# Last sums of the spectral filter's pairs 6 and 7 in layer 2 by TensorE, and a new order of the loads, in a two-layer spectral and dense kernel

## The chip, the cores and the metric

One core of a Trainium2 chip runs the whole program. The metric is the device time of one execution in microseconds, taken as the median of several runs.

## The reference

The input has 2048 rows of 448 values in bfloat16. Two layers are the same, each a spectral part (A) and a dense part (B) with a residual.

```python
def _A_ref(x, w_r, w_i):
    X = rfft2(x.astype(float32), axes=(-2, -1))
    X = X * (w_r + 1j * w_i)
    y = irfft2(X, s=(S, D), axes=(-2, -1)).astype(bfloat16)
    return y

def _B_ref(x, w1, b1, w2, b2):
    h = x @ w1 + b1
    r = where(h > 0, h, 0)
    return (r * r) @ w2 + b2

x = x + _A_ref(_layernorm(x), w_r, w_i)
x = x + _B_ref(_layernorm(x), w1, b1, w2, b2)
x = x + _A_ref(_layernorm(x), w_r, w_i)
x = x + _B_ref(_layernorm(x), w1, b1, w2, b2)
```

S is 2048, D is 448, the dense part's width is 1792. The filter w has one complex value for each of the 2048 x 225 frequencies; its first column does not matter, as the mean is taken out.

## The kernel before

Rows are held as 128 partitions by 16 tiles. The Fourier transform over the 2048 rows is split into 16 x 128, so that all of it is matrix multiplication with constants. The stages of a spectral part are:

- first_A or second_A: a tile of x, times a constant matrix FA scaled by the row's normalisation factor (Fs), goes to XA. GpSimd and ScalarE scale in layer 1; GpSimd also makes a reversed copy of x for it (xr, held in VT).
- stage_TD: the transform over the 448 columns, constants TD in layer 1 and TQ in layer 2, result U.
- stage_B: the rest of the transform over the rows, constants G, result EF. From here on the 16 parts of the first split are taken in pairs p = 1 to 7, and pair 0 apart. A pair p has the complex spectra of two conjugate row groups.
- stage_W: the filter. For pairs, VectorE multiplies EF by w (rows tmp<-arena,Wt), subtracts and adds the products (T[3], rows tmp<-tmp), and forms the difference and the sum of the two conjugate halves, the "last sums" (rows arena<-tmp), which are written to Z. Pair 1 is done alone, the pairs 2 and 3, 4 and 5, 6 and 7 together, and pair 0 last.
- stage_Bi: the inverse over rows, for a pair two passes (even and odd columns, lb). In a pass, four matmuls have a 128 x 128 part of Z as the stationary operand and 256 columns of the constant H as the moving one. The result is copied from PSUM to VT by ScalarE or VectorE: 1024 elements at once for pairs 1 to 5 (MERGE), 512 for a pass of the pairs 6 and 7, and twice 256 for a pass of pair 0.
- stage_TI and stage_AI: the inverse over columns and the rest of that over rows; then the residual is added (L1146), the normalisation follows (ln_B), and yT holds x transposed: by matmuls for tiles 0 and 1, by DMA transposes on SP's queue for the others.

The dense part (h_part, h_pairs, o_tile) is long runs of matmuls, with ReLU on ScalarE, the square on VectorE, and the residual by VectorE's scalar_tensor_tensor (L1292). The last tile's output comes in two parts, 336 and 112 columns, and each part is stored by its own DMA.

Every engine runs a list written out by hand: ORDER holds, for each engine, numbers of units in the order in which they run. A unit is one instruction, or a group of matmuls that write one tile of PSUM, numbered in the order in which the program creates them. All waits follow from the data. Where TensorE would idle for long, matmuls on a tile of ones are put in (L1415). These numbers are of use below (numbering of before):

- SP: 3, 6, 8, 10 are x loads of two tiles each (tiles 0, 4, 8 and 12 first); 4 is FA, 28 TD, 30 GN (negated G), 29 G for the pairs, 36 and 37 the filter for pair 0, 31 and 32 the filter for the pairs, 38 TI, 33 and 35 H, 44 to 47 the dense weights, 269 TQ. ScalarE's queue loads the other four pieces of x.
- VectorE, layer 1: 167, 168, 200 copy 448 elements of U, 172 copies 448 of EF, 186 copies 896 of U; 173 is the first filter step; 246 the last. 258, 260, 262 copy 512 elements to VT, and 266, 268 twice 256.
- ScalarE, layer 1: 319, 337, 357, 375, 393, 411 are copies of 896 elements for stage_TI, 305 one for tiles 2 and 3; 279 and 283, 296 and 300 copy yT of tiles 0 and 1.
- Layer 2: 922 to 929 are the eight filter steps of pairs 6 and 7 (928 and 929 the last sums), 934 to 937 those of pair 0. Matmul units 948 and 950 are pair 6, 952 and 954 pair 7, 956 and 958 pair 0; the copies to VT after them have the next number up.
- The end: matmul units 1342, 1345, 1348 are tiles 12, 13 and 14, and 1351 and 1354 the 336 and 112 columns of tile 15.

Two helpers issue nearly all that the profile shows: matmuls have line 681, copies from PSUM 706 (ScalarE) or 707 (VectorE), sums and products of two tensors 735, loads 673. In the profile's names, U, EF, Z and the dense part's buffers are views of arena; yA, TIo of tmp; xr of VT; W1 and W2 are W_sb.

Of the kernel before, what the change touches and what calls it, by code (L numbers as in the profile page):

```python
# [6 lines left out]
ALU = mybir.AluOpType  # L7
# [4 lines left out]
P = 128  # L12
# [12 lines left out]
VB_PAIRS = (2, 3, 4, 5)  # L25
MERGE = (1, 2, 3, 4, 5)
# [10 lines left out]
def make_constants():  # L37
# [70 lines left out]
    return dict(GN=GN, FA=np.concatenate([FA, -FA], 1), FI=np.concatenate([FI, -FI], 1), TD=TD, G=G, H=H, TI=TI, TQ=TQ,  # L108
# [18 lines left out]
1354""",  # L127
    "act": """
# [12 lines left out]
1315 1325 1323 1330 1328 1335 1333 1338 1340""",  # L141
    "dve": """
# [24 lines left out]
    "pool": """  # L167
12 14 16 15 13 18 17 20 19 22 69 21 26 61 77 85 23 24 106 93 25 116 132 129 158 155 145 142""",
    "sp": """
3 4 6 8 36 38 10 34 31 27 35 28 29 39 30 41 32 33 37 44 47 45 40 46 314 269 334 352 354 355 372 390 408 426 1005 1026  # L170
1044 1046 1064 1082 1047 1100 1118 1250 1209 1306 1303 1203 1212 1253 1259 1300 1297 1350 1206 1347 1256 1344 1353
1356""",
}
# [1320 lines left out]
```

## Time and profile before

| | us |
|---|---|
| median of 3 runs | 266.54 |
| lowest and highest | 266.14, 266.84 |
| the profiled execution | 266.92 |
| its span, first to last instruction | 265.0 |
| TensorE busy in the span | 256.8 |
| VectorE busy | 204.5 |
| ScalarE busy | 172.7 |
| GpSimd busy | 14.2 |

The granted TensorE clock is 1.000 over the span. A matmul's busy time includes its way through the array, so matmuls that follow one another overlap; the distance of their starts is the price of one, not the mean length. In a timeline row, the first number is the start, the second the time from the first start to the last end, x the count, and the bracket holds the idle time ahead of it and what ended it.

### The profile page before, as it was taken

Reading aid. Unit: us, or ns where it says so; the run is one execution under the profiler, and the core shown is the slowest. Engines: PE = TensorE matmul, PEld = TensorE weight load, DVE = VectorE, ACT = ScalarE, POOL = GpSimd, SP = SyncE. Lnnn points to the kernel's source line nnn. Section 1 sums busy time; section 2 is a strip of 40 time slices with the busy share of each in tenths; the row PEclk is TensorE's granted clock in tenths of the full one; section 3 lists DMA queues with packets and bytes.
Section 4 is the critical chain, followed back from the end, with each engine's and each line's share of the span. In section 5 each row is a group of like instructions: output and inputs, shape, how many; then the busy total and the mean of one; then the engine's idle time right before and its main releaser. Section 6 shows DMA issues by size and latency. Waiting matters only on the chain.

```text
span 265.0 us, 5666 instructions
## 1 busy us (share of the span) xinstructions
PE 256.8 (97%) x2125; PEld 162.6 (61%) x2125; DVE 204.5 (77%) x658; ACT 172.7 (65%) x375; POOL 14.2 (5%) x32
## 2 busy tenths in 40 slices
PE   6999989999999999999999999999999999999996
PEld 2676768797544555665558756789654465554454
DVE  2978998999969983489998899899964069921662
ACT  5978897999449447893216889999634886121820
POOL 8840000000000000000000000000000000000000
PEclk9999999999999999999999999999999999999999
DMA  7999900032300214000000000022232000220053
GB/s 223 303 299 385 270 8 2 0 72 41 74 2 1 44 37 80 2 0 2 0 1 2 2 0 2 0 45 41 42 69 45 2 0 2 40 41 2 0 173 106
DMA packets 25531, 16.33 MB, mean 62 GB/s; under 512 B 18174, under 2 KB 24542, under 8 KB 25504
## 3 DMA queue, kind: packets, MB, share of 16 engines
q1 hardware_dynamic: 24768, 14.25, 19.9%
q10 hardware_dynamic: 576, 0.92, 1.0%
q0 software_dynamic: 160, 0.81, 0.9%
q8 instruction: 17, 0.28, 0.4%
q14 instruction: 10, 0.08, 0.1%
HBM read 10.46 MB, written 1.84 MB: 46 GB/s over the span
## 4 chain that ended last, share of the span: by engine, by line
PE 81%; DVE 8%; ACT 5%; DMA 2%; issue 2%; SPq 0%; POOL 0%; DVEq 0%; POOLq 0%
PE ps L681 81%; DVE tmp L735 6%; DMA xin<-in_A_x_dram 2%; DVE arena L735 2%; ACT VT L706 2%; ACT tmp L706 2%; ACT arena L706 1%; SPq L673 0%; ACT yT L706 0%; ACT mv L700 0%; DVE st L825 0%; PE ps L1415 0%; ACT Fs L717 0%; POOL Fs L718 0%; DVE VT L707 0%
## 5 line engine op out<-in xcount | busy, mean ns | idle before, releaser
L681 PE MATMUL ps<-yT,W_sb 64*128 64x512 bf16 (+1 forms) x770 | 90.3, 346 | 0.1
L681 PE MATMUL ps<-W_sb,arena 128*128 128x448 bf16 (+3 forms) x476 | 87.0, 342 | 0.0
L681 PEld LDWEIGHTS ps<-yT,W_sb 64*128 64x128 bf16 (+1 forms) x770 | 54.5, 95 | 31.9 <-ACT arena L700 1.3
L700 ACT ACTIVATE arena<-ps,b1col 128x512 bf16<-128x512 f32 x84 | 51.9, 689 | 28.8 <-PE ps L681 28.8
L681 PEld LDWEIGHTS ps<-W_sb,arena 128*128 128x128 bf16 x476 | 45.4, 98 | 38.5 <-DVE arena L735 1.5
L735 DVE TENSOR_TENSOR arena<-arena 128x512 bf16<-128x512 bf16 (+1 forms) x140 | 45.8, 366 | 24.7 <-ACT arena L700 24.5
L706 ACT ACTIVATE arena<-ps 128x448 bf16<-128x448 f32 (+1 forms) x41 | 26.0, 705 | 4.5 <-PE ps L681 4.4
L1170 ACT ACTIVATE VT<-x_sb 128x448 bf16<-128x448 bf16 x28 | 16.1, 580 | 16.4 <-DVE x_sb L1146 16.4
L700 ACT ACTIVATE mv<-mv,epst 128x1 f32<-128x1 f32 (+1 forms) x45 | 12.6, 296 | 17.0 <-DVE mv L826 14.0
L700 ACT ACTIVATE arena<-ps 128x256 bf16<-128x256 f32 x56 | 18.0, 386 | 0.6 <-PE ps L681 0.5
L706 ACT ACTIVATE XA<-ps 128x512 bf16<-128x512 f32 x26 | 14.5, 590 | 5.2 <-PE ps L681 5.1
L681 PE MATMUL ps<-arena,G_sb 128*128 128x448 bf16 (+1 forms) x84 | 16.9, 335 | 0.9 <-ACT arena L706 0.9
L1292 DVE SCALAR_TENSOR_TENSOR x_sb<-ps,mv,arena 128x448 bf16<-128x448 f32 (+2 forms) x13 | 8.3, 644 | 11.9 <-PE ps L681 11.8
L681 PE MATMUL ps<-H_sb,arena 128*128 128x256 bf16 x128 | 15.8, 273 | 1.2 <-DVE arena L735 0.6
L706 ACT ACTIVATE VT<-ps 128x1024 bf16<-128x1024 f32 (+2 forms) x20 | 14.0, 773 | 3.0 <-PE ps L681 3.0
L735 DVE TENSOR_TENSOR tmp<-arena,Wt 128x896 bf16<-128x896 bf16 x26 | 15.4, 623 | 0.6 <-ACT arena L706 0.4
L681 PE MATMUL ps<-yT,VT 64*128 64x512 bf16 x42 | 15.8, 376 | 0.0
L681 PEld LDWEIGHTS ps<-H_sb,arena 128*128 128x128 bf16 x128 | 11.7, 98 | 5.0 <-DVE arena L735 3.4
L681 PE MATMUL ps<-TD_sb,XA 112*128 112x112 bf16 (+3 forms) x232 | 14.3, 229 | 0.1
L681 PEld LDWEIGHTS ps<-TD_sb,XA 112*128 112x128 bf16 (+3 forms) x232 | 12.3, 103 | 2.8 <-ACT XA L706 0.5
L706 ACT ACTIVATE tmp<-ps 128x896 bf16<-128x896 f32 (+1 forms) x16 | 12.7, 853 | 1.1 <-PE ps L681 1.0
L681 PEld LDWEIGHTS ps<-arena,G_sb 128*128 128x128 bf16 x84 | 7.7, 98 | 6.5 <-ACT arena L706 1.5
(84 smaller groups left out, 299.6 us busy)
## 6 DMA issues: line engine op xcount, KB each, us to landing
out_dram<-x_sb SPq DMA_DIRECT2D x15, 112.0 KB, 1.8
W_sb<-in_B_w_dram SPq DMA_DIRECT2D x1, 1568.0 KB
W_sb<-in_B_w_dram SPq DMA_DIRECT2D x1, 1344.0 KB, 11.0
xin<-in_A_x_dram ACTq DMA_DIRECT2D x4, 224.0 KB, 6.4
xin<-in_A_x_dram SPq DMA_DIRECT2D x4, 224.0 KB, 8.7
H_sb<-c_H SPq DMA_DIRECT2D x1, 896.0 KB, 8.6
G_sb<-c_G SPq DMA_DIRECT2D x1, 672.0 KB, 6.9
Wt<-in_A_w_r_dram SPq DMA_DIRECT2D x1, 393.8 KB, 3.7
```

The lines of the kernel that those rows point to most:

```text
L681: return sch.add("pe", lambda e: e.matmul(_res(o), lhsT, rhs, start=start, stop=stop, skip_group_check=skip), [lhsT, rhs], [o], cost=cost, ...
L700: sch.add("act", lambda e: e.activation(o, _res(i), func, **kw), rd, [o], cost=c)
L706: op = sch.add(engs[0], lambda e: e.activation(o, _res(i), ACT.Copy) if h[0].eng == "act" else e.tensor_copy(o, _res(i)), [i], [o], cost=c ...
L735: sch.add(eng, lambda e: e.tensor_tensor(o, _res(a), b, op), [a, b], [o], cost=_free(o) / rate + 69.0)
L1170: op = sch.add("act", lambda e, i=i, o=o, x=x, h=h: e.activation(o, x, ACT.Square, accum_out=sd[:, i, 1:2]) if h[0].eng == "act" else e.sc ...
L1292: small(lambda e: e.scalar_tensor_tensor(out=o, in0=_res(i), scalar=rs[0] if rs else 1.0, in1=xi, op0=ALU.add if t >= 4 and last else ALU. ...
```

## The change

In layer 2, for pairs 6 and 7, stage_W writes the products' difference and sum (what was T[3]) straight to Z and leaves out the two last sums. stage_Bi then takes four matmuls in each pass, one for each of the four parts, with 512 columns in place of 256: the part's contribution to both halves at once, with H and a negated copy of it (HN, new rows 9 and 10 of H_sb, 256 KB) as moving operand. The four are accumulated in one PSUM tile. HN comes by a DMA of its own on SP's queue, in the first dense part. Layer 1's and the other pairs' arithmetic stays as it is.

The lists of all engines are other ones. SP's begins with x ahead of FA and of the other constants. Units after 269 have other numbers: HN is 270, so that 270 to 927 of before are one higher, and from 930 on they are one lower. The core of the diff:

```diff
--- before.py
+++ after.py
@@ -23,6 +23,7 @@
 EPS = 1e-5
 V_PAIRS = (1, 2, 3, 4, 5, 6, 7)
 VB_PAIRS = (2, 3, 4, 5)
+SD_PAIRS = (6, 7)
 MERGE = (1, 2, 3, 4, 5)
...
     GN = -G[:, [p + 1 for p in VB_PAIRS], 0]
-    return dict(GN=GN, FA=np.concatenate([FA, -FA], 1), FI=np.concatenate([FI, -FI], 1), TD=TD, G=G, H=H, TI=TI, TQ=TQ,
+    return dict(GN=GN, HN=-H[:, [p + 1 for p in SD_PAIRS]], FA=np.concatenate([FA, -FA], 1), FI=np.concatenate([FI, -FI], 1), TD=TD, G=G, H=H, TI=TI, TQ=TQ,
                 J=np.eye(P)[::-1])
...
 ORDER = {
     "pe": """
...
-942 940 946 944 938 954 950 952 948 956 958 978 961 980 963 1084 982 965 1028 995 969 1066 986 1048 997 973 1010 990
-1290 1238 1243 1304 1301 1298 1108 1295 1251 1248 1254 1257 1307 1312 1317 1322 1327 1332 1337 1345 1348 1342 1351
-1354""",
...
+941 937 931 943 945 953 951 947 957 949 955 960 1009 962 979 1065 977 964 1047 981 994 1027 985 968 1083 996 972 989
+1289 1237 1242 1107 1300 1294 1303 1253 1247 1297 1250 1256 1306 1311 1316 1321 1326 1331 1336 1344 1341 1353 1347
+1350""",
     "act": """
...
-258 268 375 319 337 393 305 411 294 277 296 279 300 283 357 310 309 431 311 429 328 438 447 450 456 435 327 441 453
...
-871 881 879 885 903 897 895 905 901 915 899 919 917 931 921 943 941 933 945 947 939 955 951 949 959 979 981 1085 1029
...
+358 338 277 306 295 278 280 376 412 310 284 311 312 394 442 430 434 436 448 454 457 463 445 329 432 451 328 466 330
...
+906 900 902 920 916 922 918 930 940 942 932 946 944 954 952 938 958 956 961 1010 978 1066 1048 995 967 986 984 1084
     "dve": """
...
-123 114 148 128 127 149 135 154 137 136 153 138 118 141 121 140 131 105 147 168 186 173 174 175 176 177 178 179 193
-180 191 192 194 196 195 214 197 216 198 215 213 218 217 230 229 234 219 220 232 231 233 235 236 237 238 243 244 245
-246 260 266 288 290 273 376 292 271 293 320 321 275 377 276 322 323 297 280 298 281 308 307 379 326 339 378 394 325
...
-886 888 877 889 876 887 890 891 909 907 893 908 892 906 911 910 924 922 912 913 923 925 927 926 928 929 934 935 936
...
+122 114 125 141 140 123 148 128 150 127 149 151 105 154 55 153 95 144 160 167 168 172 200 173 174 175 176 178 177 193
+191 180 179 194 192 195 196 197 198 215 213 214 216 218 217 230 220 219 229 232 234 231 233 235 236 237 238 243 244
+245 246 262 258 268 272 289 274 291 322 276 293 321 294 302 297 298 323 299 281 324 308 301 282 309 326 327 313 314
...
+860 870 873 874 875 876 890 887 878 888 877 889 891 892 910 907 894 893 908 909 911 912 926 913 914 923 924 925 927
+928 933 934 935 936 948 950 963 980 1012 1011 965 982 966 983 969 970 1050 971 987 988 997 998 1013 1014 1030 1068
...
     "pool": """
-12 14 16 15 13 18 17 20 19 22 69 21 26 61 77 85 23 24 106 93 25 116 132 129 158 155 145 142""",
+12 15 13 16 17 14 18 20 19 22 21 53 69 61 23 77 24 85 25 116 119 26 142 145 129 132 158 155""",
     "sp": """
-3 4 6 8 36 38 10 34 31 27 35 28 29 39 30 41 32 33 37 44 47 45 40 46 314 269 334 352 354 355 372 390 408 426 1005 1026
-1044 1046 1064 1082 1047 1100 1118 1250 1209 1306 1303 1203 1212 1253 1259 1300 1297 1350 1206 1347 1256 1344 1353
-1356""",
+3 6 4 8 10 28 30 29 36 32 40 41 39 31 27 34 45 37 33 35 44 38 46 47 315 335 353 355 356 270 373 391 269 409 427 1004
+1025 1043 1045 1046 1063 1081 1296 1208 1099 1202 1249 1117 1302 1305 1258 1252 1211 1255 1355 1299 1205 1343 1349
+1346 1352""",
...
-        H_sb = sb("H_sb", [P, 9, 2, 2 * P])
+        H_sb = sb("H_sb", [P, 9 + len(SD_PAIRS), 2, 2 * P])
...
-        dma("sp", H_sb[:, 2:], dc["H"][:, 2:])
+        dma("sp", H_sb[:, 2:9], dc["H"][:, 2:])
...
-                tt(T[3][:, 0], T[2][:, 1], T[1][:, 0], ALU.subtract)
-                tt(T[3][:, 1], T[2][:, 0], T[1][:, 1], ALU.add)
+                sd_ = not first and p0 in SD_PAIRS
+                o = z_[:, 4 * p0:4 * (p0 + n), :].rearrange("p (q e r) l -> p e q r l", e=2, r=2) if sd_ else T[3]
+                tt(o[:, 0], T[2][:, 1], T[1][:, 0], ALU.subtract)
+                tt(o[:, 1], T[2][:, 0], T[1][:, 1], ALU.add)
+                if sd_:
+                    return
                 z = z_[:, 4 * p0:4 * (p0 + n), :].rearrange("p (q s) l -> p s q l", s=4)
                 t = T[3]
...
-                    for g in range(2):
+                    if not first and p in SD_PAIRS:
+                        h, n = 2 * (p + 1), 2 * (9 + SD_PAIRS.index(p))
+                        w = H_sb[:].rearrange("p i h c -> p (i h) c")
+                        for j, (e, r, a, c) in enumerate(((0, 1, h, h + 1), (0, 0, n, h + 1), (1, 0, h + 1, h),
+                                                          (1, 1, n + 1, h))):
+                            v = w[:, a, :]
+                            v = bass.AP(v.tensor, v.offset, [v.ap[0], [(c - a) * 2 * P, 2], [1, 2 * P]])
+                            mm(q[lambda b, k=k: ps[:, b + k, :].rearrange("p (g c) -> p g c", g=2)],
+                               z[:, 2 * e + r, lb:2 * P:2], v, j == 0, j == 3)
+                    for g in range(2) if first or p not in SD_PAIRS else ():
                         for h in range(2):
                             mm(q[lambda b, g=g, k=k: ps[:, b + k, g * 256:(g + 1) * 256]],
                                z[:, 2 * g + h, lb:2 * P:2], H_sb[:, p + 1, h, :], h == 0, h == 1)
...
         sch.bias, sch.tag = PR["ramp"][0], "TQ"
         dma("sp", TQ_sb[:], dc["TQ"])
+        sch.tag = "HN"
+        dma("sp", H_sb[:, 9:], dc["HN"])
         ffn(False)
         spectral(False)
```

More of the change, by code (lines that the diff above doesn't have):

```diff
@@ L116 @@
     "pe": """
[10 rows of a table removed]
-1354""",
-    "act": """
[12 rows of a table removed]
-1315 1325 1323 1330 1328 1335 1333 1338 1340""",
-    "dve": """
[23 rows of a table removed]
-1249 1331 1329 1101 1334 1336 1339 1341 1119 1346 1349 1343 1352 1355""",
[10 rows of a table added]
+1350""",
+    "act": """
[12 rows of a table added]
+1327 1334 1332 1337 1339""",
+    "dve": """
[23 rows of a table added]
+1318 1328 1325 1335 1330 1333 1338 1340 1118 1342 1251 1354 1345 1348 1351""",
     "pool": """
-12 14 16 15 13 18 17 20 19 22 69 21 26 61 77 85 23 24 106 93 25 116 132 129 158 155 145 142""",
+12 15 13 16 17 14 18 20 19 22 21 53 69 61 23 77 24 85 25 116 119 26 142 145 129 132 158 155""",
     "sp": """
-3 4 6 8 36 38 10 34 31 27 35 28 29 39 30 41 32 33 37 44 47 45 40 46 314 269 334 352 354 355 372 390 408 426 1005 1026
-1044 1046 1064 1082 1047 1100 1118 1250 1209 1306 1303 1203 1212 1253 1259 1300 1297 1350 1206 1347 1256 1344 1353
-1356""",
+3 6 4 8 10 28 30 29 36 32 40 41 39 31 27 34 45 37 33 35 44 38 46 47 315 335 353 355 356 270 373 391 269 409 427 1004
+1025 1043 1045 1046 1063 1081 1296 1208 1099 1202 1249 1117 1302 1305 1258 1252 1211 1255 1355 1299 1205 1343 1349
+1346 1352""",
 }
```

73 rows, old and new, of the table ORDER are left out of this document.

## The prediction

> **What bounds the kernel now.** I began with the page's first part and then read the chain of waits in order of time, because TensorE's share alone says nothing about where it waits.
>
> ```profile
> PE 256.8 (97%) x2125; PEld 162.6 (61%) x2125; DVE 204.5 (77%) x658; ACT 172.7 (65%) x375; POOL 14.2 (5%) x32
> ```
>
> ```profile
> 13.83 13.38 PE ps L681 x123
> ...
> 50.17 94.14 PE ps L681 x765
> ...
> 148.29 1.18 DVE tmp L735 x2
> ...
> 160.57 1.72 PE ps L681 x14
> ...
> 162.31 4.33 ACT VT L706 x6
> ...
> 166.78 3.48 PE ps L681 x41
> ...
> 172.41 90.27 PE ps L681 x685
> ...
> 262.70 0.33 DVE x_sb L1292
> ```
>
> Each row is start, length, engine, written tile, line. Two long rows, 94.14 and 90.27 us, are the two feed-forward parts: TensorE runs there without a wait, so no new order can shorten them; it can only add a wait. What can be won or lost lies between them: the start, the spectral part of layer 1 (about 14 to 50 us), that of layer 2 (144 to 172) and the last store. In layer 2's spectral part the chain is on VectorE from 148.29 to 160.57, goes over matmuls and ScalarE's copies into VT, and is back on TensorE at 166.78. So I read this stretch by engine in the timeline.
>
> ```profile
> 161.50 1.16 DVE L735 TENSOR_TENSOR tmp<-tmp 128x896 bf16<-128x896 bf16 x2
> 162.70 1.16 DVE L735 TENSOR_TENSOR arena<-tmp 128x896 bf16<-128x896 bf16 x2
> 163.78 1.16 DVE L735 TENSOR_TENSOR tmp<-arena,Wt 128x896 bf16<-128x896 bf16 x2
> 164.85 0.69 DVE L735 TENSOR_TENSOR arena<-tmp 128x448 bf16<-128x448 bf16 x2
> ```
>
> ```profile
> 158.09 1.91 PE L681 MATMUL ps<-H_sb,arena 128*128 128x256 bf16 x16
> ...
> 163.38 3.15 PE L681 MATMUL ps<-H_sb,arena 128*128 128x256 bf16 x24 [0.23 <-DVE arena L735]
> 163.92 2.62 PE L681 MATMUL ps<-H_sb,arena 128*128 128x256 bf16 x22
> ```
>
> The second and third rows of the last fence come from answers with different windows: the 24 matmuls of pairs 6, 7 and 0 began at 163.38, and 22 of them ran from 163.92 to 166.54. The DVE row at 162.70 is the pair of last sums of pairs 6 and 7, which the change removes; the rows at 163.78 and 164.85 are pair 0. TensorE waited for the sums, then had enough to do until 166.54.
>
> **The filter step, part by part.** *Removed:* two VectorE sums. Two rows follow one another at 162.70 and 163.78, so the pair costs 1.08 us, and it lies on the chain. *Added:* each of the 16 matmuls of pairs 6 and 7 gets 512 columns for 256. A 256-column one costs, by the row of 16 and its own length below, (1.91 - 0.27) / 15 = 0.109 us. No row here has this operand with 512 columns; the nearest is the 448-column output matmul.
>
> ```profile
> L681 PE MATMUL ps<-H_sb,arena 128*128 128x256 bf16 x128 | 15.8, 273 | 1.2 <-DVE arena L735 0.6
> ```
>
> ```profile
> 237.66 3.57 PE L681 MATMUL ps<-W_sb,arena 128*128 128x448 bf16 x18
> ```
>
> ```profile
> L681 PE MATMUL ps<-W_sb,arena 128*128 128x448 bf16 x420 | 81.3, 353 | 0.0
> ```
>
> (3.57 - 0.35) / 17 = 0.189 us for 448 columns. By columns 512 gives 0.216 us. So 16 cost 3.46 us where they cost 1.74: +1.72 us of TensorE for -1.08 us of VectorE, at a place where both take turns on the chain. The bounds for one matmul are 0.189 (the 448 row) and 0.218 (twice the 256 row); I take 0.216, as 448 is nearest.
>
> The Trainium skill, "TensorE: Matmul & The Clock Gate", section "Back-to-back issue gap", says that a sustained stream of load and matmul pairs runs at about 131 ns for 512 columns. The trace disagrees: its stream of 448 columns already takes 189 ns each. By the page the addition would be 16 x (0.131 - 0.109) = 0.35 us, an estimate from its figure.
>
> Now the times. The sums that remain end at 162.57 (the row at 161.50 has two, one each 0.54), the first of the two at 162.04. Two matmuls of the first unit need only the first, so they run at about 162.15; the other 14 start at 162.75 and take 14 x 0.216 = 3.02, to 165.77, and pair 0's eight, 0.87, between them (its input is now ready by 164.4). The last starts at 166.53 and ends at 166.81, where it ended at 166.54: +0.27. The 1.08 us given up by VectorE is thus wholly eaten by the wider matmuls.
>
> Behind it come the copies into VT. The new lists give the last unit (pair 0) to ScalarE, as two copies of 256, and leave VectorE two of 512 from pair 6.
>
> ```profile
> 162.31 4.92 ACT L706 ACTIVATE VT<-ps 128x1024 bf16<-128x1024 f32 x8 [0.41 <-PE ps L681]
> ```
>
> ```profile
> L706 ACT ACTIVATE VT<-ps 128x256 bf16<-128x256 f32 x2 | 0.7, 381 | 0.0
> ```
>
> In before, ScalarE was behind with its eight copies and released the next stage at 166.65. Now it is waiting for the last matmul at 166.81 and needs 0.38 for the first copy, so the next stage starts near 167.25 for 166.78: **+0.45 us**. Bounds: +0.27 (only TensorE's end counts) and +1.2 (two copies of 0.38 more, wholly behind it). A gain is excluded while 512 columns cost over 0.189 us and VectorE starts its filter no earlier than 148.29. It does start there by my reading: two copies of the first units go from ScalarE to VectorE and one back, +-0.3 us, taken as nothing; if this cover is gone the 0.3 shows in full.
>
> The added constants are one more DMA on SP's queue, put ahead of the transposes of tiles 8 to 15. SP has nothing else to issue there, and the tiles feed matmuls tens of microseconds later, so it is costed at nothing; the wide matmuls' new wait for it ends in layer 1 already. If that cover is gone, a wait such as VectorE's for a transpose shows (below).
>
> **The start.** SP's queue before:
>
> ```profile
> 1.17 0.42 SPq L673 DMA_DIRECT2D FA_sb<-c_FA  x1
> 1.64 0.90 SPq L673 DMA_DIRECT2D xin<-in_A_x_dram  x2
> 2.58 0.68 SPq L673 DMA_DIRECT2D Wt<-in_A_w_r_dram  x1
> 3.30 0.61 SPq L673 DMA_DIRECT2D TI_sb<-c_TI  x1
> 3.96 0.45 SPq L673 DMA_DIRECT2D xin<-in_A_x_dram  x1
> ```
>
> ```profile
> 12.76 0.56 POOL L707 COPY VT<-xin 128x448 bf16<-128x448 bf16 x1 [0.91 <-DMA xin<-in_A_x_dram]
> 13.29 3.21 POOL L718 TENSOR_SCALAR Fs<-FA_sb,rstd 128x256 bf16<-128x256 bf16 x7
> ```
>
> ```profile
> 13.51 0.61 DVE L825 BATCH_NORM_STATS2 st<-xin 128x6 f32<-128x448 bf16 x1
> ...
> 19.55 0.62 DVE L707 CAST arena<-ps 128x448 bf16<-128x448 f32 x1 [1.54 <-PE ps L681]
> 20.39 1.09 DVE L707 CAST arena<-ps 128x896 bf16<-128x896 f32 x1 [0.21 <-PE ps L681]
> 21.78 0.69 DVE L735 TENSOR_TENSOR tmp<-arena 128x448 bf16<-128x448 bf16 x2 [0.30 <-ACT arena L706]
> ```
>
> The fourth x load stands behind two constants; GpSimd waited 0.91 us for it, and seven scaled filters (3.21 us) were queued behind that copy, which feed the last matmuls of the first stage. With x first, that wait can go: bounds 0 and -0.91. Late next is VectorE, whose last statistics end at 14.1 however early x is, and the filter constant FA, which now goes behind one more x load (+0.47 us of issue). I take **-0.75**.
>
> Against it stands VectorE before its first filter step at 21.78. Old: two copies, 0.62 + 1.09 us. New: four of 448 elements, 2.48 us. The +0.77 is partly hidden by its idle 1.54 and 0.21; bounds 0 and +0.77, I take **+0.35**. At the end of layer 1 VectorE has two copies of 512 in place of one after its last sum:
>
> ```profile
> 41.57 1.35 DVE L707 CAST VT<-ps 128x512 bf16<-128x512 f32 x3
> ```
>
> Three (512, 256, 256) take 1.35 there; one more of 512 is about 0.55, and part of it runs while pair 0's matmuls run: **+0.2**, bounds 0 and 0.55. The start and layer 1 together: -0.2.
>
> **The last store.** The old list ends with the 112-column part of the last tile, the new one with its 336-column part.
>
> ```profile
> L1292 DVE SCALAR_TENSOR_TENSOR x_sb<-ps,mv,arena 128x336 bf16<-128x336 f32 x1 | 0.6, 568 | 1.3 <-PE ps L681 1.3
> ...
> L1292 DVE SCALAR_TENSOR_TENSOR x_sb<-ps,mv,arena 128x112 bf16<-128x112 f32 x1 | 0.3, 334 | 0.1
> ```
>
> ```profile
> out_dram<-x_sb SPq DMA_DIRECT2D x1, 84.0 KB, 1.6
> ...
> out_dram<-x_sb SPq DMA_DIRECT2D x1, 28.0 KB, 1.4
> ```
>
> TensorE ends at the same point, then 0.57 - 0.33 and 1.6 - 1.4: **+0.4**, bounds +0.2 and +0.5. Nothing hides it.
>
> **The new orders elsewhere.** All five lists are other ones. The two long TensorE rows have no wait to lose, so this term has one sign. The nearest measure is the wait of TensorE's weight loads for VectorE:
>
> ```profile
> PEld ps L681 <- DVE arena L735: 4.9, 11, 0.9
> ...
> DVE arena L718 <- DMA yT<-arena: 2.7, 1, 2.7
> ```
>
> Eleven waits of up to 0.9 us, and one of 2.7 on VectorE behind a transpose. I allow **+0.4** between 0 and 0.9 (one such wait, anywhere).
>
> **Sum.** -0.2 + 0.45 + 0.4 + 0.4 = +1.05. The profiled execution has a span of 265.0 us and took 266.92, so 1.9 lie around it; it is 0.38 above the median of 266.54. On the profile: 267.97. On the median: 267.6.
>
> **The rivals.** *One: every term comes out at its low end (faster).* If the spacing of these matmuls is set by the weight load and not by the columns, 512 cost the same 0.109 us as 256, and the sixteen end 14 x 0.107 = 1.5 us sooner than above. Then ScalarE bounds the stage: it may start 0.54 earlier than its 162.31, because one product (half of a row of 1.16) now stands behind the sums that feed it, and has one 256 copy more before the release, 0.29 by spacing; 166.64 - 0.54 + 0.29 = 166.4 for 166.78, so -0.4 for +0.45. With the whole 0.91 of GpSimd's wait, nothing given back at 21.78, no wait in the long rows and 0.2 for the last store: -0.9 - 0.4 + 0.2 = -1.1, 265.4. It decides once 512 columns cost under about 0.15 us. The Trainium skill's figure above stands on this side of that point. Against it: 0.189 for 448. For a gain even at the full price: constants moved up to follow x may end waits that I did not see. Chance 0.23 for the faster side.
>
> *Two: the pieces cancel.* The start keeps its 0.75 with nothing lost at 21.78, the long rows stay without a wait: -0.75 + 0.2 + 0.45 + 0.4 = +0.3, 266.8. Chance 0.27, all within 0.3%. VectorE's idle 1.54 before its copies speaks for it. The change would then do what it says and still move nothing.
>
> *Three: a ramp breaks.* In layer 1, ScalarE's list now has two of the wide copies for the inverse transform between the normalisation's yT copies. The same kind in layer 2:
>
> ```profile
> 169.46 1.73 ACT L706 ACTIVATE tmp<-ps 128x896 bf16<-128x896 f32 x2 [0.26 <-PE ps L681]
> ```
>
> If TensorE's first feed-forward matmuls, at 50.17, wait for both, they cost 1.73 in place of the 0.4 allowed: 268.9. Chance 0.1.
>
> **How the numbers follow.** A measurement of this kernel tells about 0.3%, 0.8 us, from no change: 265.74 to 267.34 is "the same". The forecast, 267.6 with 267.2 to 268.2 of its own from the bounds on its terms, has 0.4; I put nearly all of that above 267.34, and the small part below is about what rival two holds. Faster 0.23, same 0.28, slower 0.49. The range reaches down to 265.5, next to rival one, and up to 268.8, just short of rival three, and leaves out some two in ten.
>
> **What would show it.** In the profile after: 16 matmuls from H_sb with two 256 groups each, about 0.216 us apart, from 162.2 on; the first TI matmul 0.45 us later, counted from VectorE's first filter step; GpSimd's wait of 0.91 gone and VectorE's first filter step at 21.4 in place of 21.78; a last scalar_tensor_tensor of 336 columns. Wrong, if the two long TensorE rows start earlier by over a microsecond, if the wide matmuls are spaced by under 0.17 us, or if a new wait of TensorE over 1 us stands in the feed-forward parts.

## The result and the profile after

The changed kernel took 270.43 us (median of 4, 270.04 to 270.96), the kernel before 266.34 (median of 4 on the same chip): a ratio of 1.0149, interval 1.0131 to 1.0168, so 4.1 us slower. Forecast were 267.6 and a range up to 268.8: the direction held, the size was four times too small.

The first part of the page, after:

```profile
PE 257.6 (96%) x2124; PEld 163.1 (61%) x2125; DVE 205.0 (76%) x660; ACT 169.0 (63%) x371; POOL 14.2 (5%) x32
```

VectorE lost two sums of the filter, and yet it has two instructions more and 0.5 us more work: the new lists moved copies from ScalarE to it, which has four instructions and 3.7 us of work less. TensorE has 0.8 us more work in a span 4.0 us longer, so it stood still more. Where, the chain of waits says (start, length, engine and written tile, line):

```profile
182.93 36.11 PE ps L682 x290
219.04 0.02 issue
219.07 2.42 ACT arena L701 x4
221.49 0.56 ACT VT L1184 x2
222.04 0.59 ACT arena L701
222.63 0.14 issue
222.77 43.21 PE ps L682 x284
265.98 0.02 issue
266.00 0.57 DVE x_sb L1306
```

In before, one piece of 90.27 us of TensorE ran from 172.41 to the end. Here that row is broken: from 219.07 to 222.77 the chain lies on ScalarE. (Lines are up to 16 further down than in before: 681 is 682, 735 is 736, 1292 is 1306.)

To see every place I cut the executions at the same events: the first TD matmul, the first inverse-column matmul (TI), the first feed-forward matmul (FF), the first matmul of 64 rows (64) and VectorE's first filter step of layer 2 (W2). Each length is a difference of two starts in the timelines, one execution of each kernel; the two columns of experiments are told below. "Filter alone" is the new filter in the old lists, "orders alone" the new lists with the old filter.

| from, to (us) | before | filter alone | orders alone | after |
|---|---|---|---|---|
| TD, TI of layer 1 | 24.90 | 24.90 | 25.45 | 25.45 |
| TI, FF | 7.52 | 7.51 | 7.50 | 7.50 |
| FF, 64 | 24.67 | 24.67 | 25.51 | 25.51 |
| 64, W2 | 73.45 | 73.45 | 73.73 | 73.73 |
| W2, TI of layer 2 | 18.49 | 19.27 | 19.16 | 18.92 |
| TI, 64 | 31.38 | 32.15 | 31.47 | 31.69 |
| 64, TensorE's end | 64.50 | 64.50 | 65.45 | 65.45 |
| TensorE's end, end of span | 2.33 | 2.31 | 2.78 | 3.01 |

The filter's own stretch grew by 0.43. The other rows grew by 0.55 + 0.84 + 0.28 + 0.31 + 0.95 + 0.68 less 0.02, 3.6 us. The first TD matmul stands at 17.75 in before and at 17.71 after.

The filter stretch of layer 2, after (timeline):

```profile
163.06 1.16 DVE L736 TENSOR_TENSOR arena<-tmp 128x896 bf16<-128x896 bf16 x2
163.97 4.38 PE L682 MATMUL ps<-H_sb,arena 128*128 128x512 bf16 x23 [0.57 <-DVE arena L736]
164.13 1.16 DVE L736 TENSOR_TENSOR tmp<-arena,Wt 128x896 bf16<-128x896 bf16 x2
168.38 0.66 ACT L707 ACTIVATE VT<-ps 128x256 bf16<-128x256 f32 x2 [0.53 <-PE ps L682]
```

As forecast, the remaining sums feed the wide matmuls, pair 0's products follow at once, and ScalarE waits for the last matmul.

The first and the second wait of TensorE in the feed-forward parts, from the timeline of after (the bracket holds the idle time and what ended it):

```profile
57.57 0.54 PE L682 MATMUL ps<-tmp,FI_sb 128*128 128x224 bf16 x4 [0.56 <-ACT arena L701]
...
220.38 1.51 PE L682 MATMUL ps<-yT,W_sb 64*128 64x512 bf16 x12
222.77 0.54 PE L682 MATMUL ps<-tmp,FI_sb 128*128 128x224 bf16 x4 [0.88 <-ACT arena L701]
```

The same place in before:

```profile
218.05 1.51 PE L681 MATMUL ps<-yT,W_sb 64*128 64x512 bf16 x12
219.49 7.74 PE L681 MATMUL ps<-W_sb,arena 128*128 128x448 bf16 x40
```

The matmuls on FI_sb are stage_AI units: number 398 (tiles 12 and 13 of layer 1) and 1108 (tiles 14 and 15 of layer 2), in before's numbering. The operands (tmp) are VectorE's, but ScalarE's ReLU (L701) ended the wait. The code gives a reason: matmuls write to PSUM, which has eight banks, and a unit of stage_AI for two tiles claims two neighbouring ones, which must both have been read. In the new list, 1108 stands right behind the last units of the first dense matrix, 398 behind units of the same kind, and by the trace a bank of the pair that each gets had just been written by them: each unit starts 0.15 to 0.2 us after the end of a ReLU on such a result. In before, three output tiles of one bank each stood ahead of 1108. ScalarE is not later than in before: its last three ReLUs begin 0.03 us after the group's last matmul has ended, in before 1.16 us after it.

```profile
220.16 0.59 ACT L1170 ACTIVATE VT<-x_sb 128x448 bf16<-128x448 bf16 x1
220.63 0.22 ACT L1170 ACTIVATION_READ_ACCUMULATOR VT<-x_sb 128x1 f32 x1
220.72 1.86 ACT L700 ACTIVATE arena<-ps,b1col 128x512 bf16<-128x512 f32 x3
```

```profile
221.36 0.59 ACT L1184 ACTIVATE VT<-x_sb 128x448 bf16<-128x448 bf16 x1
221.83 0.22 ACT L1184 ACTIVATION_READ_ACCUMULATOR VT<-x_sb 128x1 f32 x1
221.92 1.86 ACT L701 ACTIVATE arena<-ps,b1col 128x512 bf16<-128x512 f32 x3
```

The first of these fences is before's ScalarE, the second after's; L1170 and L1184 are the square and sum of a normalisation. In before the three ReLUs ran while TensorE was already on its output tiles, since 219.49.

### The profile page after: what moved, and what is told of

Its sections match the earlier page's. It is cut to its first block, busy times and chain, and to the rows that moved or that the text cites. A ratio compares the mean times of both kernels' runs of the same rounds, so it can differ in the third digit from the quotient of the medians.

```text
span 269.0 us, 5645 instructions
## 1 busy us (share of the span) xinstructions
PE 257.6 (96%) x2124; PEld 163.1 (61%) x2125; DVE 205.0 (76%) x660; ACT 169.0 (63%) x371; POOL 14.2 (5%) x32
## 5 line engine op out<-in xcount | busy, mean ns | idle before, releaser
L701 ACT ACTIVATE arena<-ps,b1col 128x512 bf16<-128x512 f32 x84 | 52.1, 691 | 35.1 <-PE ps L682 35.0
L707 ACT ACTIVATE arena<-ps 128x448 bf16<-128x448 f32 (+1 forms) x38 | 25.3, 724 | 5.6 <-PE ps L682 5.6
L1184 ACT ACTIVATE VT<-x_sb 128x448 bf16<-128x448 bf16 x29 | 16.9, 588 | 12.9 <-DVE x_sb L1160 12.9
L701 ACT ACTIVATE mv<-mv,epst 128x1 f32<-128x1 f32 (+1 forms) x45 | 12.3, 294 | 13.7 <-DVE mv L827 13.1
L707 ACT ACTIVATE XA<-ps 128x512 bf16<-128x512 f32 (+1 forms) x27 | 14.2, 584 | 9.0 <-PE ps L682 9.0
L701 ACT ACTIVATE arena<-ps 128x256 bf16<-128x256 f32 x56 | 17.7, 394 | 2.1 <-PE ps L682 1.8
L682 PE MATMUL ps<-H_sb,arena 128*128 128x256 bf16 (+1 forms) x127 | 17.0, 286 | 1.5 <-DVE arena L736 1.4
L682 PE MATMUL ps<-tmp,FI_sb 128*128 128x224 bf16 (+1 forms) x72 | 10.7, 270 | 1.8 <-ACT arena L701 1.4
```

What stands on the lines that cost most here:

```text
L682: return sch.add("pe", lambda e: e.matmul(_res(o), lhsT, rhs, start=start, stop=stop, skip_group_check=skip), [lhsT, rhs], [o], cost=cost, ...
L701: sch.add("act", lambda e: e.activation(o, _res(i), func, **kw), rd, [o], cost=c)
L707: op = sch.add(engs[0], lambda e: e.activation(o, _res(i), ACT.Copy) if h[0].eng == "act" else e.tensor_copy(o, _res(i)), [i], [o], cost=c ...
L1184: op = sch.add("act", lambda e, i=i, o=o, x=x, h=h: e.activation(o, x, ACT.Square, accum_out=sd[:, i, 1:2]) if h[0].eng == "act" else e.sc ...
```

## The experiments

All times are medians; "before" is the kernel before on the same chip. In brackets stand the ratio to it and its 95% interval. Unit numbers are before's, HN is the load of the negated constants.

**The two halves.** The old lists with the new filter, HN's DMA put behind the old unit 355; and the new lists with the old filter, the two sums behind those that feed them:

```diff
 dve (old):  ... 926 927
-928 929
 934 ...
 sp (old):   ... 355
+HN
 372 ...
```

> The filter change alone: the old lists of all engines, without the two last sums and with one more DMA for the negated constants. Theory A (the new orders cost nearly all): between VectorE's first filter step of layer 2 and the first inverse-transform matmul there are 18.5 us before and 18.9 after, so the filter alone costs about 0.4 us: 266.8, between 266.4 and 267.2. Theory B (the wide matmuls and what hangs on them cost most of the 4 us, partly hidden from that stretch): 269 or more.

> The new orders alone: the new lists of all engines with the old filter, its two last sums put right behind the step before them. Theory A: the new orders cost 3.5 us and more, 269.6 to 270.4. Theory B: the orders are harmless, 267.0 or less.

The filter alone took 267.53 (before 266.53; ratio 1.0034, 1.0020 to 1.0047), the orders alone 270.09 (1.0133, 1.0111 to 1.0154). So 3.6 of the 4.1 us come with the lists. (The two halves, 1.0 and 3.6 us, add up to more than the whole.) The filter alone overshot its range by 0.3: its own stretch lost 0.78, as TensorE now has one run of 64 H matmuls (the 16 wide ones among them) with no wait in which the added width could hide, and behind it TensorE waited 0.44 for a transpose.

```profile
157.40 9.39 PE L682 MATMUL ps<-H_sb,arena 128*128 128x256 bf16 x64
...
181.06 2.79 PE L682 MATMUL ps<-yT,W_sb 128*128 128x256 bf16 x24 [0.44 <-DMA yT<-x_sb]
```

That transpose is issued some 9.3 us after the first TI matmul. In before, in the orders alone and in two more kernels without HN it landed 3.0 to 3.1 us later. In the changed kernel it took 4.76, and TensorE's weight load (PEld) waited for it:

```profile
182.93 1.10 PEld L682 LDWEIGHTS ps<-yT,W_sb 128*128 128x128 bf16 x11 [0.29 <-DMA yT<-x_sb]
```

It was late in eight of the ten kernels that load HN. In the ninth (layer 1 in the old order, below) it took 3.08, and in the tenth the trace doesn't show its landing. HN's own load lies tens of microseconds earlier, in a part whose length it doesn't change (24.67 in the table). What delays the transpose is not settled.

**x first alone.** The old lists and filter, five places of SP's list changed. As in the changed kernel, FA (4) stands behind the second load of x:

```diff
-3 4 6 8 36 38 10 34 31 ...
+3 6 4 8 10 36 38 34 31 ...
```

> Only SP's queue is changed in the kernel before: the four loads of x and FA go first, as in the new list (x, x, FA, x, x), the rest keeps its old order. If GpSimd's wait of 0.91 us for the fourth load was on the path, as the prediction had it: about 0.75 faster, 265.6. Rival: VectorE's statistics end no earlier, because they are back to back and x only changes who waits: within 0.2 us of before.

265.88 against 266.53: ratio 0.9981, interval 0.9968 to 0.9994, a gain of 0.65 us, by the interval between 0.2 and 0.85. This is the one part of the change that was seen to pay by itself, and it is faster than both kernels. GpSimd's wait of 0.91 is gone, 0.18 stands in its place:

```profile
12.71 2.92 POOL L718 TENSOR_SCALAR Fs<-FA_sb,rstd 128x256 bf16<-128x256 bf16 x6 [0.18 <-DVE mv L826]
```

**The old end.** The changed kernel with the matmuls, the sum and the store of the last tile's 112 columns at the end of the lists, as in before.

```diff
 pe:  ... 1345 1342
-1354
 1348 1351
+1354
```

> The changed kernel with the 112-column part of the last tile moved back to the end of TensorE's, VectorE's and SP's lists; nothing else is changed. The spans differ by 4.0 us and the last matmul's end by 3.3, so the end has 0.7: theory A expects 0.5 to 0.7 back, 269.8. If the store order of the other tiles is what costs there, and not the width of the last piece: 0.2 or less, 270.3.

270.37 (1.0146, 1.0125 to 1.0167) for 270.43: nothing gained. The lengths say why. From TensorE's end to the end of the span it is 3.44 us, for 3.01, as the last store now has to wait for SP:

```profile
260.92 5.87 SPq L674 DMA_DIRECT2D out_dram<-x_sb  x10
...
264.26 1.02 DVE L1306 SCALAR_TENSOR_TENSOR x_sb<-ps,mv,arena 128x336 bf16<-128x336 f32 x2 [1.31 <-PE ps L682]
```

The last sum has ended at 265.28, and SP issues stores until 266.79. In before the last store's issue ends 0.38 us after the last sum. So this run doesn't tell what the width of the last piece costs; the stores stand in the way.

**Two units placed later.** The changed kernel, 398 behind four more units of the next group, 1108 behind three output tiles, the sums 1109 and 1110 and one ReLU (1239) moved with it:

```diff
 pe:  ... 437 449
-398
 464 467 485 479
+398
 506 ...      ... 1238 1243
-1108
 1301 1295 1304
+1108
 1254 ...
```

> The changed kernel with two TensorE units placed later and nothing else of the new lists undone: the inverse of tile 12 in layer 1 goes four units back (behind four more of the first feed-forward product), that of tile 14 in layer 2 behind the three output tiles o8, o10, o11, as in the kernel before; its two VectorE sums and one ReLU of ScalarE follow. Theory A (each of these units writes a pair of PSUM banks and stood where no pair had been read yet, so that TensorE stood still for 0.56 and 0.88 us): both waits go, the part from the first feed-forward matmul to the first of 64 rows falls from 25.51 to about 24.7 us and the last part of layer 2 from 65.49 to about 64.6; 270.43 - 0.84 - 0.95 = 268.6, range 268.3 to 269.0. Rival B (ScalarE's ReLUs are simply late there, whichever unit stands at the place): the next unit takes over the wait, 270.0 to 270.5.

268.21 (before 266.43; 1.0067, 1.0053 to 1.0080): the distance to before fell from 4.09 to 1.78, a little more than expected. FF to 64 fell to 24.79, the last part to 64.51. Both units now run without a wait:

```profile
57.80 0.55 PE L682 MATMUL ps<-tmp,FI_sb 128*128 128x224 bf16 x4
...
220.30 3.96 PE L682 MATMUL ps<-W_sb,arena 128*128 128x448 bf16 x20
```

Nothing took the wait over: the one-bank units that now stand there run without a wait. So it was the place of these two units and not ScalarE; that it is the second bank that they wait for follows from the code and from what ended the wait.

**Old copies and old stores on top.** The same, with the copies 167, 172, 200 back on ScalarE and 186 on VectorE, and the last units of TensorE and VectorE and all stores of SP in the old order.

> The changed kernel with the two units placed later as in the run sent with this one, and also the old owners of four copies in the first stage (three back to ScalarE, one to VectorE) and the old order of the last stores. The new filter, x first and the rest of the new lists stay. Theory A (the loss is the sum of these places): 268.6 less 0.6 for VectorE's first filter step (4.64 us after the first TD matmul falls to about 4.05) less 0.3 for the end: 267.7, range 267.3 to 268.2. Rival: the start is late for another reason (transfers that arrive in another order), the stretch stays at 4.6 and the time at 268.3 to 268.7.

272.71 (1.0235, 1.0221 to 1.0248): a miss, but in two parts that can be read apart. At the end it is this mixture's own fault: stores that wait for late sums came to stand in SP's queue ahead of the last two transposes, two ahead of each, and the 64-row part took 69.47 us for 64.51. The rows show the second pair:

```profile
240.24 3.47 SPq L674 DMA_DIRECT2D out_dram<-x_sb  x2
243.76 1.23 SPq L669 DMA_TRANSPOSE yT<-arena  x1
245.04 24.18 SPq L674 DMA_DIRECT2D out_dram<-x_sb  x13
```

At the start the owners of the copies do half of what was expected (VectorE's first filter step 4.34 us after the first TD matmul, for 4.64 and an expected 4.05), and it is worth nothing: the first TI matmul still comes 25.44 us after it. The end, with the last piece and all stores in the old order, takes 2.31 us from TensorE's last matmul, for 2.33 in before.

**Another place for the trade.** Pairs 2 and 3 for 6 and 7, in the old lists, pair 1's matmuls moved into TensorE's gap:

```diff
-SD_PAIRS = (6, 7)
+SD_PAIRS = (2, 3)
 pe (old):  ... 920
+938
 932 942 940 946 944
-938
```

> The kernel before with its own lists, but the last sums of pairs 2 and 3 (not 6 and 7) by TensorE, and pair 1's matmuls and copy put one place earlier, into TensorE's gap that now holds four filler matmuls on ones. If the trade loses only because pairs 6 and 7 are the last to be summed and TensorE then has 1.72 us more behind the sums, here the sums of pairs 4 to 0 come 1.08 us earlier, TensorE has 0.87 us of pair 1 done in the gap, and its last matmul of the stretch ends 0.3 to 0.6 us earlier than before: 266.0, range 265.8 to 266.3. Rival (TensorE bounds the whole stretch whichever pair is chosen, so the added 1.72 us count): 267.0 to 267.8.

267.02 (before 266.43; 1.0018, 1.0006 to 1.0031): slower, at the rival's figure, and half by its reason. VectorE, relieved of 1.08 us, waited 0.86 of it for ScalarE's copy of EF:

```profile
157.75 1.17 DVE L736 TENSOR_TENSOR tmp<-arena,Wt 128x896 bf16<-128x896 bf16 x2 [0.86 <-ACT arena L707]
```

The chain of waits is no longer on VectorE here. It lies on TensorE with the wide matmuls, and then on ScalarE's copies:

```profile
155.29 6.04 PE ps L682 x36
161.33 0.02 issue
161.35 1.02 ACT VT L707
162.37 0.81 ACT arena L707
163.18 3.33 ACT VT L707 x5
166.51 0.09 issue
166.60 1.49 PE ps L682 x16
```

So most of what VectorE was relieved of there was room that it then spent waiting. The stretch took 18.71 for 18.49, only 0.22 more. The transpose behind it was late again (TensorE waited 0.54), and from TI to 64 it is 32.10 for 31.38, so that transpose costs this kernel more than the stretch does.

**The new filter with the new lists in layer 2's spectral part alone**, in the old lists otherwise.

> The new filter in the kernel before's lists, with the new lists' order for layer 2's spectral part alone (last forward transform of tile 15 to the first inverse tile). The prediction's term for this stretch, +0.45, was made with these lists: then 266.53 + 0.4 = 266.95, range 266.7 to 267.2, and the stretch from VectorE's first filter step to the first inverse-column matmul is 18.9 us. Rival (the wide matmuls cost what they cost in the old order, the new order gives nothing back): 19.3 us in the stretch and 267.3 to 267.7, as with the filter alone in the old order (267.53).

267.75 (1.0050, 1.0037 to 1.0064). The stretch is the 18.93 expected; the time is not, as 0.9 us went at the seam behind it, where the new order ends and the old one goes on (TI to 64: 32.31 us, with waits of TensorE for VectorE of 0.47 and 0.22).

**What was left.** On top of the two units: layer 1's spectral part in the old order on TensorE, ScalarE and VectorE; the sum of o5 and the 112-column store moved; and both.

```diff
 dve: ... 1258
+1252
 ... 1119 1343
-1252
 sp:  ... 1256
-1356
 1300 1206 1344 1350 1347
+1356
 1353
```

> The kernel with the two units placed later (268.21), and layer 1's spectral part from the first TD matmul to the last Bi copy put back into the old order with the old owners, on TensorE, ScalarE and VectorE; the loads, the first stage before it and all behind it stay new. Theory A (the 0.55 us that the stretch from the first TD matmul to the first inverse-column matmul is longer, 25.45 for 24.90, come from the order of the units in it: the new one puts two pairs' H matmuls ahead of the last pair's G matmuls, and TensorE waits 0.78 us there for VectorE): the stretch is 24.9 and the time 267.65, range 267.4 to 267.9. Rival (the stretch is longer because its inputs come in another order from the stage before): 25.3 or more and 268.1 to 268.4.

> The kernel with the two units placed later (268.21), with VectorE's sum of output tile o5 moved from the end of its list to behind that of o7, where its matmuls are done, and the store of the last tile's 112 columns put just before the last store on SP's queue. Theory A (the new lists let the sum of o5 wait until 258 us, its store stands in SP's queue ahead of nine others, and ten stores of 28 to 112 KB then go out within 5 us, so that the last lands late): SP issues them spread out, the time from TensorE's last matmul to the end falls from 2.9 to 2.4, and the time is 267.7, range 267.5 to 267.9. Rival (the end is only the last piece's own sum and store, 336 columns for 112): 268.1 to 268.4.

> Both of the above. What then is left of the new lists against the kernel before is x first (-0.65), the filter stretch (+0.43), 0.27 in the part with the forward transforms of layer 2 and 0.3 behind the filter: theory A 268.21 - 0.55 - 0.5 = 267.15, range 266.8 to 267.5. Rival (the pieces don't add, since each later stage gives the time back as a wait): 267.6 or more.

They took 268.48, 268.44 and 268.06, before 266.74 beside them (1.0082, 1.0061 to 1.0102; 1.0075, 1.0059 to 1.0092; 1.0059, 1.0043 to 1.0075). By time none can be told from the distance of the two units alone: the last is 1.32 above before, for 1.78, and the intervals overlap. The lengths say more. Layer 1 with the old order takes 25.23: TensorE's wait of 0.78 is gone, but 0.33 of the 0.55 is still there, and it is there early on. After, layer 1:

```profile
19.69 0.94 PE L682 MATMUL ps<-TD_sb,XA 128*128 128x224 bf16 x8 [0.22 <-ACT arena L707]
...
32.62 1.04 PE L682 MATMUL ps<-H_sb,arena 128*128 128x256 bf16 x8
33.50 0.81 PE L1431 MATMUL ps<-ones 128*128 128x512 bf16 x3
35.09 1.05 PE L682 MATMUL ps<-H_sb,arena 128*128 128x256 bf16 x8 [0.78 <-DVE arena L736]
35.97 0.93 PE L682 MATMUL ps<-arena,G_sb 128*128 128x224 bf16 x8
```

The first row, stage_TD's fifth unit (185), is where the 0.33 arises. Its result is copied as 896 elements, so it too claims two banks. In before it ran on without a wait, 1.66 us after the first TD matmul (it is matmuls 33 to 40 of this row):

```profile
17.75 2.60 PE L681 MATMUL ps<-TD_sb,XA 128*64 128x224 bf16 x40
```

In all nine kernels with the new list of the first stage it starts after 1.98, when ScalarE's first copy of U has ended, also where layer 1 has the old order; in all five with the old list after 1.66. So a third wait of the kind of 398's and 1108's is the likely cause: the new first stage left other banks free. No run undid it. As for the 0.78: in before the G matmuls of 224 columns (pair 0, which feeds VectorE's last steps) stood ahead of the second group of H matmuls, and TensorE waited 0.32 and 0.40 us in that part. The stores: SP's queue in after, and then with the sum of o5 moved,

```profile
261.97 5.20 SPq L674 DMA_DIRECT2D out_dram<-x_sb  x10
```

```profile
259.04 5.55 SPq L674 DMA_DIRECT2D out_dram<-x_sb  x5
```

show the jam taken away, and the last store goes out 0.03 us after the last sum, as in before. The time from TensorE's end to the end of the span only fell from 2.86 to 2.74, against 2.33 in before. So the rival holds: what is left, 0.41, is the last piece's own sum (0.57 for 0.33) and the way of its store from there to the end (2.14 for 1.96).

**The old filter in these lists.** The last kernel with the two sums back on VectorE.

```diff
 dve: ... 927
+928 929
 934 ...
-HN (sp)
```

> The lists of the last run (both undone: the two units, layer 1's spectral part, the stores), but with the old filter: the two last sums of pairs 6 and 7 are back on VectorE, right behind the sums that feed them, and the negated constants and their DMA are gone. It tells what the filter alone is worth in lists that were made for it; the last run stood 1.32 us above the kernel before. Theory A (the prediction's own term: the trade costs 0.45 us wherever it stands, since 1.72 us of TensorE replace 1.08 of VectorE on the chain): 0.9 above before, 267.3 to 267.6, and the stretch from VectorE's first filter step of layer 2 to the first inverse-column matmul is 18.5. Rival (the lists cost that much, and in them the trade saves about 0.24, as 19.16 and 18.92 us for that stretch in the runs with the new lists say): 1.5 above before, 268.0 to 268.4, and the stretch is 19.15.

268.71 (before 266.64; 1.0077, 1.0058 to 1.0096). The stretch is 19.16, a hundredth from what the rival said, so in lists made for it the trade saves 0.24 us there. But it doesn't reach the end: from TI to 64 this kernel takes 31.47, the one with the new filter 31.68, since the transpose landed after 3.02 us for 4.76. From the first TD matmul to TensorE's end the two differ by 0.03 (in the changed kernel and the orders alone, by 0.02). The times, 2.07 above before for 1.32, agree in sign with the stretch; the intervals are too wide for more.

## Why the prediction was wrong

**The filter step, +0.45: right, +0.43.** The step by step is borne out: counted from VectorE's first filter step, the wide matmuls start after 14.07 us (13.86 forecast), the last unit's copy begins after 18.48 and the next stage starts after 18.92 (18.96 forecast). The price of a matmul of 512 columns is as taken from the 448 row. From the run with pairs 2 and 3, which has all sixteen (group of the line; count, busy, mean ns):

```profile
L682 PE MATMUL ps<-H_sb,arena 128*128 128x512 bf16 x16 | 3.6, 379 | 0.0
```

(3.6 - 0.38) / 15 = 0.215 us. This is where rival one would have decided, and its figure of 0.131 from the Trainium skill ("TensorE: Matmul & The Clock Gate", section "Back-to-back issue gap") is not seen. The same section has a formula, columns / 2.4 + 2.5 ns, which it holds for too long in a stream; it gives 216 ns, and the run agrees with it. What the prediction did not see is that the +0.43 is a difference of two things: the new lists alone cost +0.67 in this stretch (19.16), and the trade then gives 0.24 back, which the late transpose behind it takes again. HN's load, put at nothing, did cost nothing where it is issued; whether it has to do with that transpose is open.

**The start, -0.75: right as a mechanism, about right in size; how much the new lists keep is not settled.** x first alone gave 0.65. In the new lists GpSimd's wait of 0.91 is gone, but 0.79 for a statistic of VectorE stands in its place, and VectorE in turn waits 0.87 for x:

```profile
10.88 1.15 DVE L826 BATCH_NORM_STATS2 st<-xin 128x6 f32<-128x448 bf16 x2 [0.87 <-DMA xin<-in_A_x_dram]
```

```profile
12.25 0.93 POOL L719 TENSOR_SCALAR Fs<-FA_sb,rstd 128x256 bf16<-128x256 bf16 x2 [0.79 <-DVE m L840]
```

The first TD matmul came at 17.71, at 16.68 to 17.22 in the nine other kernels that load x in this order (16.81 with x first alone), and at 17.07 to 17.75 in the four that do not. These are single executions. The five kernels with the changed kernel's lists up to there have 16.68, 16.92, 17.07, 17.22 and 17.71, so its own 17.71 is the latest of a wide scatter, and a part of the gain may well be kept.

**Layer 1, +0.35 and +0.2: the sum right (+0.55), the place wrong, so the sum is luck.** VectorE's first filter step did come late, at 22.35 where 21.4 was named, and 0.62 later than in before when counted from the first TD matmul. But only 0.29 of that are the copies, and giving them back moved nothing behind it. TensorE's order of H and G matmuls accounts for 0.22 of the 0.55; the other 0.33 is the wait of the fifth TD unit for ScalarE's copy, which the prediction didn't have.

**The last store, +0.4: +0.68**, of which 0.41 by its reason: with the stores freed, the longer sum and the longer store are all that is left. The rest is the jam in SP's queue, which the prediction didn't look at: in the changed kernel the last store went out 0.21 us after its sum, with the stores freed 0.03 us after it.

**The new orders elsewhere, +0.4 with a bound of 0.9: this is the step that failed.** It measured 0.84 + 0.28 + 0.31 + 0.95 = 2.4 us (0.2 of the 0.31 is the transpose that landed late). The bound was one wait of the size of VectorE's waits in before, "anywhere". But the lists stood in the diff, and they could have been walked: 398 and 1108 stand there behind units that fill PSUM, and each needs a pair of banks. Before's trace had no such wait from which to take a price, but it had the price of clearing a bank, ScalarE's row of three ReLUs at 220.72 (1.86, so about 0.6 each). Undoing just these two took back 2.3 of the 4.1 us (1.7 by the lengths). The rule is in the Trainium skill too ("Perfetto Trace Analysis", section "Matmuls"): groups should rotate through PSUM banks so that the clearing of one lies beside the next one's matmuls; the 0.88 us is what it cost here where the rotation had come round. The 0.28 ahead of layer 2 is two smaller waits of TensorE for VectorE:

```profile
144.66 0.40 PE L682 MATMUL ps<-Fs,tmp 128*128 128x128 bf16 x4 [0.16 <-DVE tmp L745]
...
145.47 0.41 PE L682 MATMUL ps<-Fs,tmp 128*128 128x64 bf16 x8 [0.20 <-DVE tmp L745]
```

No run undid it.

**The rivals.** One (faster) needed wide matmuls at the price of narrow ones: no. Two (all cancels) needed nothing lost before VectorE's first filter step and no wait in the long rows; neither held. Three was right that a ramp would break and wrong where: from TI to FF, where ScalarE's wide copies stand, the time is 7.50 for 7.52. The tests named for the text's own failure were too coarse: none of the new waits is over 1 us, and together they cost more than twice the forecast.

With the lists cleaned as far as was tried, 1.3 us remain. The lengths of that kernel account for them as layer 1 0.33, ahead of layer 2 0.27, the filter stretch 0.43, the end 0.40, the late transpose 0.2 and 0.3 in smaller pieces, 1.9 in all, less about 0.6 us at the start (an estimate: what the lengths leave over).

## What to carry to other kernels

When a change brings a whole new order, cost the order and not only the idea: walk the new list of the busiest engine and ask at each unit that claims more than one buffer who last wrote them and how long they take to be cleared. Cutting both traces at the same ten events finds such losses, and splitting the change into its halves tells which one to look at. Before work is taken off an engine, look at what that engine waits for next: here VectorE, relieved of 1.08 us in the middle pairs, waited 0.86 us for ScalarE right behind them, and the time didn't fall.

## What the runs showed of the hardware

Most lengths between events reproduce to some 0.02 us from kernel to kernel where the lists are the same (25.45 in five kernels, 73.72 to 73.73 in nine). The exception is a length in which TensorE waits for a transpose: 31.47 or 31.68 from TI to 64, as it lands 3.0 or 4.76 us after its issue. Most of the scatter lies ahead of the first TD matmul, at 16.68 to 17.71 us in five kernels with the same lists up to there, while the loads arrive. Differences of under 0.5 us are better read from such lengths than from medians.

A unit that claims two banks can wait for one that was just written: 0.56 and 0.88 us of TensorE's time here, gone when each was put behind four other units or three output tiles of one bank.

A store that waits in SP's queue holds up all that stands behind it: two ahead of each of the last two transposes cost 5 us of TensorE's time (69.47 for 64.51).
